# Second pair's slopes after the first pair's sine, its second chunk summed by a matrix of ones, and the copied product first

## The chip, the cores and the metric

The kernel runs on one core of one Trainium2 chip. The metric is the device time of one execution in microseconds; lower is better. The engines are named as the profile names them: PE is TensorE's matmul, PEld its weight load, DVE is VectorE, ACT is ScalarE, POOL is GpSimd, and SP issues the DMAs.

## The reference, cut to what matters

```python
# attention: a decayed linear recurrence per (batch, head), 768 steps, head size 48
mag = sqrt(a_re^2 + a_im^2);  scale = min(mag, 0.999) / (mag + 1e-6)
a = (a_re + i a_im) * scale
for t in range(768):
    S = a[t] * S + outer(k[t], v[t])        # S complex, the outer product real
    y[t] = q[t] @ real(S)
# first expert layer: 1536 tokens, 384 -> 2048 -> 384, softplus between
x = softplus(y_rows @ w_in) @ w_out
# second expert layer: 4 experts, 384 -> 1024 -> 384, relu between, weighted by p
out = sum_e p[:, e] * (relu(x @ w1[e]) @ w2[e])
```

The kernel does the recurrence in chunks of 128 steps: phases and log magnitudes are summed along time by a matmul with a triangular matrix, and a chunk is then scores, a mix with V, and a state for the next chunk.

## The kernel before

There are two batches of six chunks. A **pair** n is two chunks, c = 0 and 1, that share their activations: pairs 0 to 2 are batch 0, pairs 3 to 5 batch 1. One pair's front is: `squares` (L533: two squares on ScalarE, their sum on VectorE for pair 0, on GpSimd for the others), `ratio` (L539: Ln and Exp on ScalarE, then four VectorE operations that give a slope), `arctan` (L555), `logmag` (L548: Ln, Exp and two VectorE operations), `prefix` (L559: sums along time on TensorE), `wrap` and `level` (L587, L593: the results out of PSUM), `trig` (L623: Abs and two Sin). `decay` (L637) and `s3_units` (L645) then form the scaled queries and keys, transpose them on TensorE, and compute the chunk.

`prefix(n, c, what)` sums angles (what = 0) or log magnitudes (what = 1). For pair 0 the second chunk gets the first chunk's total from an additional matmul with a matrix of ones (L582). For all others `carry` (L603) fetches the last row of the chunk before with two small DMAs, and a GpSimd addition puts it into the first row of the next chunk (L564) before the triangular matmul. `s2_units` (L611) lists this chunk after chunk.

Ln and Exp lie in one table of ScalarE, Sin and Arctan in another. `excursion` (L717) loads the second table, runs what it is given, and loads the first one again. Before the change the first excursion holds the arctan of pairs 0 and 1 and the sine of pair 0 (`trigs0`, L777); the second one holds the sine of pair 1 and the arctan of pair 2.

What the program text says is put into each engine's own row by a scheduler at build time. An engine then works through its row in order: an instruction that waits holds up all behind it. Since the scheduler decides, some instructions stand elsewhere than the text has them.

From about 50 us on, the tokens go through the expert layers, in products of 128 x 384 on TensorE. Six of the twelve steps (`FAST`, second half of the run) use a form with eleven products in place of twelve (`part`, L407): four in q == 0 (px, two into pc, pv), three in q == 1, two in q == 2 and two in q == 3. In q == 0 ScalarE copies pc to `ha` (L437) and pv to `he` (L441), and VectorE adds px to `ha` (L438). The first product of q == 1 adds into pv, so it waits for the copy `he`; the third adds into px, so it waits for the addition to `ha`. A second-layer product (nine matmuls, L319) stands between two parts. Checks of the inputs (`look`, `look_w`, L887 and L901) run beside this: a DMA into a buffer of the ring `raw`, two ScalarE operations (L906, L907), one on VectorE. Weight loads use the same ring of four.

Of the kernel before, what the change touches and what calls it, by code (L numbers as in the profile page):

```python
# [15 lines left out]
ALU = mybir.AluOpType  # L16
# [59 lines left out]
def fast_path(ctx: ExitStack, tc, bad, wsc, qkv, a_re, a_im, w_in, w_out, probs, w1, w2, out):  # L76
    nc = tc.nc
# [327 lines left out]
    grp = {}  # L405

    def part(k, j, q):  # L407
        b = k // 6
        raws, sums = W[k, 2 * j]

        def prod(ps, w, x, start=False, stop=False):
            lt, li = (raws, w) if w < 5 else (sums, w - 5)
            for n, (p, r) in enumerate(((0, 0), (1, 0), (0, 1))):
                rhs = XC[b][:, r, x, :] if isinstance(x, int) else halves(b, *x, r)
                nc.tensor.matmul(ps, lt[:, p, li, :], rhs, start=(start and n == 0), stop=(stop and n == 2),  # L415
                                 skip_group_check=True)

        def keep(nm):
            return late["u"].tile([P, WM], F32, tag="h", name=f"{nm}{k}_{j}", bufs=3)

        def activate(f, blk, h):
            nm = f"{k}_{blk}_{f}"
            pool = tmp if blk == 0 else late["g"]
            g = pool.tile([P, 2, WM], F32R, tag="g", name="g" + nm, bufs=GB)
            nc.scalar.activation(g[:, 0, :], h, AF.Relu)
            nc.vector.scalar_tensor_tensor(g[:, 1, :], h, 0.0, g[:, 0, :].bitcast(F32), ALU.max, ALU.subtract)
            g_t[k, blk, f] = g

        if q == 0:
            x = grp["x"] = psum.tile([P, 512], F32, tag="h", name=f"px{k}_{j}", bufs=2)[:, :WM]  # L430
            c = psum.tile([P, 512], F32, tag="a", name=f"pc{k}_{j}", bufs=3)[:, :WM]
            v = grp["v"] = psum.tile([P, 512], F32, tag="a", name=f"pv{k}_{j}", bufs=3)[:, :WM]
            prod(x, 7, (1, 0), True, True)
            prod(c, 3, 0, True)
            prod(c, 4, (2, 0), False, True)
            h = keep("ha")
            nc.scalar.copy(h, c)  # L437
            nc.vector.tensor_tensor(h, x, h, ALU.add)  # L438
            prod(v, 9, (0, 1), True, True)
            e = grp["e"] = keep("he")  # L440
            nc.scalar.copy(e, v)  # L441
            activate(2 * j + 1, 0, h)
        elif q == 1:
            x, v = grp["x"], grp["v"]
            prod(v, 0, 3)
            prod(v, 2, (2, 0), False, True)
            h = keep("hb")
            nc.scalar.copy(h, v)
            prod(x, 8, 2, False, True)
            nc.vector.tensor_tensor(h, x, h, ALU.add)  # L450
            activate(2 * j, 0, h)
        elif q == 2:
            x, e = grp["x"], grp["e"]
            prod(x, 2, (2, 1))
            prod(x, 1, 4, False, True)
            nc.vector.tensor_tensor(e, x, e, ALU.add)
            activate(2 * j, 1, e)
        else:
            x = grp["x"]
            prod(x, 5, (2, 1))  # L460
            prod(x, 6, 1, False, True)
            activate(2 * j + 1, 1, x)
# [70 lines left out]
    def squares(n, sl):  # L533
        R, I, T1, T2 = (wide(t, sl) for t in st[n])
        nc.scalar.activation(T1, R, AF.Square)
        nc.scalar.activation(T2, I, AF.Square)
        (nc.vector if n == 0 else nc.gpsimd).tensor_tensor(T2, T1, T2, ALU.add)

    def ratio(n, sl):  # L539
        R, I, T1, T2 = (wide(t, sl) for t in st[n])  # L540
# [14 lines left out]
    def arctan(n):  # L555
        I = wide(st[n][1], slice(0, 2))
        act(I, I, AF.Arctan)

    def prefix(n, c, what):  # L559
        cc = (CH[n] + c) % CB  # L560
        src = st[n][1 if what == 0 else 3]
        if cc > 0 and n != 0:
            row = src[0:1, c, :]
            nc.gpsimd.tensor_tensor(row, rows[0][0:1, what, :], row, ALU.add)  # L564
        ps = psum.tile([P, 512], F32, tag="a", name=f"{'pf' if what == 0 else 'pl'}{n}_{c}", bufs=3)
# [11 lines left out]
            st[n, c, what] = ps  # L577
            return nc.tensor.matmul(ps[:, :HD], tri_r, lo, start=False, stop=True)
        t, lo = ((trik, onek), (tri, ones))[what]
        prev = range(c) if n == 0 else ()  # L580
        for i in prev:
            nc.tensor.matmul(ps[:, :HD], lo, src[:, i, :], start=(i == 0), stop=False)  # L582
        mm = nc.tensor.matmul(ps[:, :HD], t, src[:, c, :], start=(len(prev) == 0), stop=True)
# [25 lines left out]
        nc.sync.dma_start(rows[0][0:1, 1, :], dlam[127:128, :])  # L609

    def s2_units(n):  # L611
        units = []
        for c in range(2):
            units.append(lambda c=c: (prefix(n, c, 0), prefix(n, c, 1)))
            units.append(lambda c=c: (wrap(n, c), level(n, c)))
            if (CH[n] + c) % CB < CB - 1:
                units.append(lambda c=c: carry(n, c))
        return units
# [98 lines left out]
    def excursion(*parts):  # L717
        def run():
            use_table(TRIG)
            for f_ in parts:  # L720
                f_()
            use_table(LOGEXP)
        return run

    both = slice(0, 2)
# [43 lines left out]
        ratio(0, one[c])  # L769
    level(0, 0)  # L770
    decay(0, 0)
    squares(1, both)
    ratio(1, both)
    level(0, 1)
    decay(0, 1)

    def trigs0():  # L777
        arctan(0)
        for c in range(2):
            prefix(0, c, 0)  # L780
            if c == 0:
                arctan(1)
            wrap(0, c)
            if c == 1:
                carry(0, 1)
            trig(0, one[c])

    excursion(trigs0)()

    base = [0] + [24 + 16 * i for i in range(12)]  # L790
    ring = []
# [357 lines left out]
```

## Time and profile before

| | |
|---|---|
| median of 3 runs | 737.78 us (737.22 to 738.26) |
| the profiled execution | 738.36 us |
| its span, first to last instruction | 736.6 us |
| mean granted clock of TensorE | 0.988 of full |
| PE busy / PEld busy | 95% / 92% |
| DVE busy / ACT busy / POOL busy | 80% / 66% / 4% |

A page of the profile gives busy time by engine; the trace gives each instruction with its start, its duration, the idle time of its engine just before it, and what ended that. A busy share is an average over stages. This run has three: a start in which TensorE has little to do, a stretch in which attention and the first expert layer are mixed, and a long one of expert layers.

### The profile page before, as it was taken

To read this page: it belongs to the slowest core of one execution; us is meant where nothing else is said; L and a number is where in the kernel's file an instruction comes from. 1 tells how busy PE (TensorE), PEld (TensorE's weight loads), DVE (VectorE), ACT (ScalarE), POOL (GpSimd) and SP (SyncE) were. 2 spreads that over 40 slices of the span, in tenths; PEclk is the share of its full clock that TensorE was granted. 3 is DMA by queue.
4 is the path that set the end of the run, shared out by engine and by line. 5 is a ranking of instruction groups with operands and counts; after the bars stand their busy time and mean duration, and the time that the engine had idled before them with its cause. 6 is when DMAs were issued, how large, how long until landed. Compare 5 with 4: busy or idle time off the path is not lost.

```text
span 736.6 us, 13285 instructions
## 1 busy us (share of the span) xinstructions
PE 702.5 (95%) x5159; PEld 674.9 (92%) x5159; DVE 586.4 (80%) x1149; ACT 487.4 (66%) x898; POOL 32.3 (4%) x31
## 2 busy tenths in 40 slices
PE   2789999999999999999999999999999999999996
PEld 1468899999899999999999999999999999999996
DVE  6999999955875854548888779988778898998963
ACT  7887976888896856345686665555556567766640
POOL 1122010000111001000000000000000000000000
PEclk9699999999999999999999999999999999999998
DMA  7665666621211420121022120213445345455401
GB/s 268 195 191 179 201 203 192 224 77 44 86 45 59 122 80 2 59 86 44 23 86 65 43 87 21 87 44 109 119 157 155 127 151 172 150 172 152 162 31 69
DMA packets 36342, 83.56 MB, mean 113 GB/s; under 512 B 4528, under 2 KB 13232, under 8 KB 36272
## 3 DMA queue, kind: packets, MB, share of 16 engines
q1 hardware_dynamic: 36272, 82.64, 35.5%
q8 instruction: 42, 0.69, 0.4%
q14 instruction: 28, 0.23, 0.1%
HBM read 73.95 MB, written 8.65 MB: 112 GB/s over the span
## 4 chain that ended last, share of the span: by engine, by line


## 5 line engine op out<-in xcount | busy, mean ns | idle before, releaser
L232 PE MATMUL h<-X,A 128*128 128x384 f32 (+1 forms) x936 | 175.9, 329 | 2.3 <-ACT A L181 0.8
L232 PEld LDWEIGHTS h<-X,A 128*128 128x128 f32 x936 | 153.4, 188 | 5.6 <-issue 1.6
L319 PE MATMUL y<-B,g 128*128 128x384 f32 x744 | 150.2, 335 | 0.2 <-DVE acc L350 0.2
L319 PEld LDWEIGHTS y<-B,g 128*128 128x128 f32 x744 | 131.0, 188 | 0.7 <-issue 0.5
L319 PE MATMUL y<-g,B 128*128 128x384 f32 (+1 forms) x504 | 91.0, 315 | 0.3 <-ACT g L285 0.3
L319 PE MATMUL z<-B,g 128*128 128x384 f32 x372 | 84.7, 334 | 0.0
L319 PEld LDWEIGHTS y<-g,B 128*128 128x128 f32 x504 | 79.3, 189 | 2.0 <-ACT g L285 0.6
L319 PEld LDWEIGHTS z<-B,g 128*128 128x128 f32 x372 | 66.3, 188 | 0.0
L247 ACT ACTIVATE e<-h 128x384 f32<-128x384 f32 (+1 forms) x60 | 30.8, 512 | 37.1 <-PE h L232 36.0
L250 DVE SCALAR_TENSOR_TENSOR e<-h,e 128x384 f32<-128x384 f32 (+1 forms) x60 | 34.9, 581 | 20.6 <-ACT e L103 19.8
L255 DVE SCALAR_TENSOR_TENSOR g<-h,g 128x384 fp32r<-128x384 f32 x32 | 17.7, 555 | 28.1 <-ACT g L254 28.1
L103 ACT ACTIVATE e<-e,b_one 128x384 f32<-128x384 f32 (+1 forms) x60 | 38.2, 637 | 1.3
L103 ACT ACTIVATE e<-e 128x384 f32<-128x384 f32 (+1 forms) x60 | 32.8, 547 | 1.3
L415 PE MATMUL px<-X,sA 128*128 128x384 f32 x144 | 33.4, 340 | 0.0
L319 PE MATMUL z<-g,B 128*128 128x384 f32 x144 | 32.9, 335 | 0.0
L415 PE MATMUL px<-XC,sA 128*128 128x384 f32 x144 | 32.8, 336 | 0.0
L664 PE MATMUL tp<-ident,QK 128*96 128x128 f32 x192 | 27.2, 288 | 5.7 <-DVE QK L655 4.6
L664 PEld LDWEIGHTS tp<-ident,QK 128*96 128x96 f32 x192 | 22.2, 133 | 10.3 <-DVE QK L655 6.2
L254 ACT ACTIVATE g<-h 128x384 fp32r<-128x384 f32 x32 | 15.6, 488 | 21.3 <-PE h L232 21.1
L286 DVE TENSOR_TENSOR g<-e,g 128x384 fp32r<-128x384 f32 x48 | 26.6, 555 | 3.7 <-ACT g L285 2.9
L480 ACT CAST B<-rawB 128x768 fp32r<-128x768 f32 x24 | 20.0, 834 | 14.4 <-DMA rawB<-in_w_dram 7.3
L350 DVE SCALAR_TENSOR_TENSOR acc<-y,pr,acc 128x384 f32<-128x384 f32 x46 | 26.3, 612 | 1.7 <-PE y L319 1.7
(204 smaller groups left out, 1416.7 us busy)
## 6 DMA issues: line engine op xcount, KB each, us to landing
rawA<-in_w_dram SPq DMA_DIRECT2D x32, 384.0 KB, 3.0
rawB<-in_w_dram SPq DMA_DIRECT2D x32, 384.0 KB, 3.1
rawA<-in_w_in_dram SPq DMA_DIRECT2D x16, 384.0 KB, 3.5
rawB<-in_w_out_dram SPq DMA_DIRECT2D x16, 384.0 KB, 3.8
chkw<-in_w_in_dram SPq DMA_DIRECT2D x16, 384.0 KB, 3.2
chkw<-in_w_out_dram SPq DMA_DIRECT2D x16, 384.0 KB, 3.2
qk<-in_qkv_dram SPq DMA_DIRECT2D x12, 384.0 KB, 3.4
v<-in_qkv_dram SPq DMA_DIRECT2D x12, 256.0 KB, 2.9
```

Of the source, the lines that this page charges most:

```text
L103: i = nc.scalar.activation(out_, in_, fn, **kw)
L232: nc.tensor.matmul(ps, wt[:, p, kk, o:o + P], XB[b][:, q, kk, tok], start=(n == 0), stop=(n == 3 * KT - 1))
L247: nc.scalar.activation(t, h, AF.Abs)
L250: nc.vector.scalar_tensor_tensor(t, h, 0.0, t, ALU.max, ALU.add)
L254: nc.scalar.activation(g[:, 0, :], h, AF.Relu)
L255: nc.vector.scalar_tensor_tensor(g[:, 1, :], h, 0.0, g[:, 0, :].bitcast(F32), ALU.max, ALU.subtract)
L286: nc.vector.tensor_tensor(g[:, 1, :], t, g[:, 0, :].bitcast(F32), ALU.subtract)
L319: mm = nc.tensor.matmul(ys[j], l_, r_, start=(opens and n == 0 and not mate), stop=(closes and n == 2), skip_group_check=k == 0)
L350: nc.vector.scalar_tensor_tensor(dst, ys[j], pcol, dst, ALU.mult, ALU.add)
L415: nc.tensor.matmul(ps, lt[:, p, li, :], rhs, start=(start and n == 0), stop=(stop and n == 2), skip_group_check=True)
L480: nc.scalar.copy(hi, src)
L664: nc.tensor.transpose(tp[:96, hh, :], src[:, hf * 4 + hh, :], ident)
```

## The change

Three things change.

- `squares(1)` and `ratio(1)` move behind the first excursion, and `arctan(1)` gets an excursion of its own behind them: two more loads of ScalarE's tables. The sum of pair 1's squares moves from GpSimd to VectorE.
- Pair 1's second chunk gets the first chunk's total by a matmul with ones, as pair 0 does. Its two GpSimd row additions and the `carry` between its two chunks go. `s2_units(1)` now takes both chunks at a time: both angle sums, both wraps, both magnitude sums, both levels, one carry.
- In `part`, q == 0, the product pv and its copy `he` come ahead of px, pc and `ha`. This applies to the 24 groups of the six FAST steps.

```diff
 part, q == 0:
+            prod(v, 9, (0, 1), True, True)
+            e = grp["e"] = keep("he")
+            nc.scalar.copy(e, v)
             prod(x, 7, (1, 0), True, True)
             prod(c, 3, 0, True)
             prod(c, 4, (2, 0), False, True)
             h = keep("ha")
             nc.scalar.copy(h, c)
             nc.vector.tensor_tensor(h, x, h, ALU.add)
-            prod(v, 9, (0, 1), True, True)
-            e = grp["e"] = keep("he")
-            nc.scalar.copy(e, v)
             activate(2 * j + 1, 0, h)
 squares:
-        (nc.vector if n == 0 else nc.gpsimd).tensor_tensor(T2, T1, T2, ALU.add)
+        (nc.vector if n < 2 else nc.gpsimd).tensor_tensor(T2, T1, T2, ALU.add)
 prefix:
-        if cc > 0 and n != 0:
+        if cc > 0 and n != 0 and (n, c) != (1, 1):
-        prev = range(c) if n == 0 else ()
+        prev = range(c) if n < 2 else ()
 s2_units:
+        if n == 1:
+            return [lambda: (prefix(1, 0, 0), prefix(1, 1, 0)), lambda: (wrap(1, 0), wrap(1, 1)),
+                    lambda: (prefix(1, 0, 1), prefix(1, 1, 1)), lambda: (level(1, 0), level(1, 1)),
+                    lambda: carry(1, 1)]
 the start:
     decay(0, 0)
-    squares(1, both)
-    ratio(1, both)
     level(0, 1)
     decay(0, 1)
 trigs0:
             prefix(0, c, 0)
-            if c == 0:
-                arctan(1)
             wrap(0, c)
     excursion(trigs0)()
+    squares(1, both)
+    ratio(1, both)
+    excursion(lambda: arctan(1))()
```

Two places where the engines' rows change. The first is ScalarE's row between the last decays of pair 0 (`dec_1`) and the second pair's arctan. Names: `im_121` and `im_130` are the slopes of pairs 0 and 1, `t_131` and `t_132` pair 1's work tiles, `pf` an angle sum, `qT` and `kT` the transposed queries and keys, `t_485` (before: `t_488`) a work tile of pair 2. Before:

```order
L597 COPY zl_128<-pl_1_159 128x384
L103 ACTIVATE t_131<-t_131,b_tiny 128x768
L103 ACTIVATE t_131<-t_131 128x768
L103 ACTIVATE dec_1_189<-zl_128 128x384 x2
L97 ACT_TABLE_LOAD
L103 ACTIVATE im_121<-im_121 128x768
L181 CAST A_0_351<-fA_0_0_383 128x384
L590 ACTIVATE t_122<-pf_0_195,b_magic 128x384
L103 ACTIVATE im_130<-im_130 128x768
```

After, from the last Sin of pair 0 on:

```order
L97 ACT_TABLE_LOAD
L103 ACTIVATE t_131<-t_131,b_tiny 128x768
L669 COPY qT_0_0_230<-tp_0_0_231 96x512
L103 ACTIVATE t_131<-t_131 128x768
L97 ACT_TABLE_LOAD
L669 COPY kT_0_0_237<-tp_0_0_238 96x512
L669 COPY qT_0_1_244<-tp_0_1_245 96x512
L181 CAST B_0_470<-fB_0_1_488 128x384
L669 COPY kT_0_1_251<-tp_0_1_252 96x512
L536 ACTIVATE t_485<-im_483 128x768
L181 CAST A_1_498<-fA_1_0_503 128x384
L103 ACTIVATE im_130<-im_130 128x768
```

Pair 1's Ln, Exp and arctan have left the row ahead of pair 0's sines; they now stand among the copies of pair 0's transposes, with a load of the table on either side, and behind one square of pair 2.

The second place is TensorE's row from the transposes (`tp`) of pair 0 to its first scores (`sp`). Before:

```order
L664 MATMUL tp_0_0_236<-ident,QK_0_221 96x128 x4
L583 MATMUL pf_0_243<-im_130,trik 128x384
L664 MATMUL tp_0_1_249<-ident,QK_0_221 96x128 x4
L664 MATMUL tp_0_1_256<-ident,QK_0_221 96x128 x4
L664 MATMUL tp_1_0_338<-ident,QK_1_325 96x128 x4
L664 MATMUL tp_1_0_345<-ident,QK_1_325 96x128
L583 MATMUL pl_0_246<-t_132,tri 128x384
L673 MATMUL sp_0_0_263<-qT_0_0_228,kT_0_0_235 128x128 x4
```

After:

```order
L668 MATMUL tp_0_0_238<-ident,QK_0_223 96x128 x4
L668 MATMUL tp_0_1_245<-ident,QK_0_223 96x128 x4
L668 MATMUL tp_0_1_252<-ident,QK_0_223 96x128 x4
L668 MATMUL tp_1_0_342<-ident,QK_1_328 96x128 x4
L668 MATMUL tp_1_0_349<-ident,QK_1_328 96x128 x4
L583 MATMUL pf_0_259<-im_130,trik 128x384
L582 MATMUL pf_1_261<-im_130,onek 128x384
L583 MATMUL pf_1_261<-im_130,trik 128x384
L677 MATMUL sp_0_0_265<-qT_0_0_230,kT_0_0_237 128x128 x4
```

Pair 1's angle sums, now three matmuls in a row, stand right ahead of pair 0's first scores.

In the FAST steps one group shows the third change. This is ScalarE's row around the copies of a group whose copy `he` stood behind two operations of a check. Before:

```order
L480 CAST B_1_6464<-rawB_1_6462 128x768
L906 ACTIVATE chkv_6494<-chkw_6493 128x384
L437 COPY ha_3_6410<-pc_3_6399 128x384
L907 ACTIVATE chkv_6494<-chkv_6494,b_mid 128x384
L441 COPY he_3_6416<-pv_3_6400 128x384
L425 ACTIVATE g_0_7_6418<-ha_3_6410 128x384
L480 CAST A_2_6516<-rawA_2_6514 128x384
```

After:

```order
L480 CAST B_1_6461<-rawB_1_6459 128x768
L435 COPY he_3_6401<-pv_3_6397 128x384
L909 ACTIVATE chkv_6491<-chkw_6490 128x384
L910 ACTIVATE chkv_6491<-chkv_6491,b_mid 128x384
L440 COPY ha_3_6412<-pc_3_6396 128x384
L425 ACTIVATE g_0_7_6415<-ha_3_6412 128x384
L480 CAST A_2_6513<-rawA_2_6511 128x384
```

The copy `he` now stands ahead of the check; the copy `ha` stands behind it. The cast of the next weights follows in both.

## Rows read from the trace of the kernel before

**Rows 1.** The page, busy time of TensorE: us (share of span) xinstructions.
```profile
PE 702.5 (95%) x5159; PEld 674.9 (92%) x5159; DVE 586.4 (80%) x1149; ACT 487.4 (66%) x898; POOL 32.3 (4%) x31
```

**Rows 2.** Stages: us, busy of PE, PEld, DVE, ACT, POOL, PEclk, DMA share, GB/s.
```profile
50.00:115.00 65.00, 60.94 (x778) 54.89 (x779) 63.72 (x113) 50.78 (x92) 8.87 (x6) 1.00 0.62 194
430.00:730.00 300.00, 299.04 (x1705) 295.52 (x1703) 254.64 (x535) 173.10 (x341) 0.00 (x0) 1.00 0.37 116
```

**Rows 3.** Timeline at the start: start, us, engine, line, operation [idle before <- releaser].
```profile
11.86 2.10 POOL L537 TENSOR_TENSOR t<-t,t 128x768 f32<-128x768 f32 x1 [10.13 <-ACT t L536]
12.33 2.04 DVE L545 TENSOR_TENSOR im<-im,re 128x384 f32<-128x384 f32 x1
12.83 0.48 ACT L597 COPY zl<-pl 128x384 f32<-128x384 f32 x1 [0.22 <-PE pl L583]
...
13.99 0.94 ACT L103 ACTIVATE t<-t,b_tiny 128x768 f32<-128x768 f32 x1 [0.69 <-POOL t L537]
...
14.96 0.84 ACT L103 ACTIVATE t<-t 128x768 f32<-128x768 f32 x1
...
16.77 1.28 ACT L97 ACT_TABLE_LOAD   x1
...
18.06 0.84 ACT L103 ACTIVATE im<-im 128x768 f32<-128x768 f32 x1
...
18.96 1.65 PE L583 MATMUL pf<-im,trik 128*128 128x384 f32 x2 [6.17 <-ACT im L103]
...
26.41 1.94 PE L664 MATMUL tp<-ident,QK 128*96 128x128 f32 x8 [3.42 <-DVE QK L655]
```

**Rows 4.** ScalarE alone, from arctan to decays: us, busy, PEclk, DMA share, GB/s.
```profile
18.06:51.00 32.94, 28.76 (x46) 0.83 0.60 184
```

**Rows 5.** Timeline around the first scores of the first pair.
```profile
27.88 1.19 POOL L564 TENSOR_TENSOR im<-rows,im 1x384 f32<-1x384 f32 x1 [13.93 <-DMA rows<-tail]
...
33.82 0.91 PE L583 MATMUL pl<-t,tri 128*128 128x384 f32 x2
...
34.57 1.95 PE L673 MATMUL sp<-qT,kT 96*128 96x128 f32 x16
...
36.07 1.82 POOL L537 TENSOR_TENSOR t<-t,t 128x768 f32<-128x768 f32 x1 [2.30 <-ACT t L536]
```

**Rows 6.** The granted clock there, microsecond by microsecond; columns as in rows 2.
```profile
32.00:33.00 1.00, 1.00 (x7) 0.96 (x6) 0.94 (x2) 0.96 (x3) 0.22 (x1) 0.53 0.88 267
33.00:34.00 1.00, 0.82 (x5) 0.38 (x4) 0.53 (x2) 0.97 (x3) 0.77 (x1) 1.00 0.87 237
```

**Rows 7.** Timeline at the first expert matmuls and second pair's decays.
```profile
49.00 0.74 PE L232 MATMUL h<-X,A 128*128 128x256 f32 x4 [0.72 <-ACT X L711]
...
49.71 1.28 ACT L97 ACT_TABLE_LOAD   x1
...
51.00 0.94 ACT L103 ACTIVATE dec<-t 128x384 f32<-128x384 f32 x2
...
55.31 1.96 PE L664 MATMUL tp<-ident,QK 128*96 128x128 f32 x16 [1.23 <-DVE QK L655]
```

**Rows 8.** Timeline, VectorE's waits after that and TensorE's last long one.
```profile
73.26 1.03 DVE L182 TENSOR_TENSOR B<-fB,B 128x384 fp32r<-128x384 f32 x2 [0.51 <-ACT B L181]
86.83 0.56 DVE L182 TENSOR_TENSOR B<-fB,B 128x384 fp32r<-128x384 f32 x1 [0.37 <-ACT B L181]
114.07 0.59 PEld L689 LDWEIGHTS yps<-A,v 128*32 128x32 f32 x24 [1.33 <-DVE A L674]
```

**Rows 9.** Waits of PEld, 430 to 600 us (total, times, longest); then the timeline.
```profile
PEld pv L415 <- ACT he L441: 1.8, 4, 0.7
...
566.55 0.55 ACT L906 ACTIVATE chkv<-chkw 128x384 f32<-128x384 int32 x1 [1.36 <-DMA chkw<-in_w_in_dram]
570.25 0.51 ACT L480 CAST A<-rawA 128x384 fp32r<-128x384 f32 x1 [1.48 <-DMA rawA<-in_w_dram]
571.88 0.48 PEld L415 LDWEIGHTS px<-X,A 128*128 128x128 f32 x3 [0.39 <-DVE hb L450]
```

## The prediction, made before the changed kernel ran

> **What bounds the kernel now.** I read the page first, for the engine with most busy time: TensorE, 95% [rows 1]. That is an average, so next come the stages. From 115 us on TensorE hardly waits; in the FAST steps it is busy 299.04 of 300 us [rows 2]. There, time can be gained only where it still waits. From 50 to 115 us VectorE is busy 63.72 of 65 us and TensorE 60.94 [rows 2]: VectorE is the tighter one, and the last long wait of TensorE, 1.33 us before 114.07, is for VectorE's mask of the scores [rows 8]. What is early or late there reaches the end in full, since nothing behind it has slack. Before 50 us TensorE waits for ScalarE and VectorE: 6.17 us for the arctan, 3.42 us for the scaled queries [rows 3]. So I ask when VectorE and TensorE come into the full stretch, that is, when the second pair's decays run (51.00) and when the first expert matmul does (49.00) [rows 7], and then what FAST gives.
>
> All sums are made against the profiled execution, 738.36 us, of which 736.6 are its span. It lies 0.58 above the median of the runs, 737.78; I carry the difference over to the median.
>
> **What is taken out before the first sine.** After the copy at 12.83 and the first pair's decays, ScalarE runs Ln (0.94) and Exp (0.84) of the second pair, the Ln after a wait of 0.69 for GpSimd's sum of squares, then the load of the table [rows 3]. Now the decays are followed by the load. The copy ends at 13.3; two decays take 0.94 [rows 7], the load 1.28: the first arctan starts at 15.5 and not at 18.06, 2.5 us earlier. VectorE has its input by then: the instruction at 12.33 took 2.04 us because GpSimd's sum ran until 13.96, and ended 0.41 after it [rows 3]; in its place stands the sum itself on VectorE, an operation with 768 columns that I estimate at 1 us from the 0.94 of such an activation [rows 3]. The 2.5 us go on through the angle sums, sines and products: the first transposes, at 26.41 before [rows 3], come at about 23.9.
>
> **What comes back behind it.** The moved work stands among the copies of those transposes. ScalarE from the first arctan to the second pair's decays was busy 28.76 us of 32.94 [rows 4], so it waited 4.2. The new row adds Ln and Exp (1.78) and two loads (2.56), and loses the copy for the removed carry (short, 0.48 like the copy at 12.83 [rows 3]): 28.76 + 3.86 = 32.6. Without waits the decays would run at 15.5 + 32.6 = 48.1, 2.9 us earlier than now. All turns on the waits.
>
> On the loads a row and a rule differ. The row: after the load at 49.71 the next activation starts at 51.00 [rows 7], and after that at 16.77 at 18.06 [rows 3], 1.29 us each time. The Trainium skill, page "ScalarE: Activation LUTs", section "What ACT_TABLE_LOAD costs", has 1283 ns for the load and some 1380 ns more for a drain, 2.66 us for each switch, and its rules ask to group activations by table, which this change does not. By the row the two loads cost 2.6 us, by the page 5.3; I take the row.
>
> The waits. Until the first wrap of an angle sum two casts of weights now stand ahead of it, and they wait for VectorE's chain of conversions, which takes as long as before: I estimate 2.5 us of waits in all up to the second arctan. That arctan ends at 34.3 by the same account: 15.5, twenty-two operations, two loads, and these waits. Its result isn't at TensorE then. GpSimd has first to add the carried row to the first chunk (1.19 [rows 5]), and ahead of it in GpSimd's row stands the sum of the third pair's squares (1.82 and 2.10 [rows 3, 5]), which waits for a square that ScalarE ends only at about 33.1, just ahead of the cast and the arctan. So GpSimd is done at 33.1 + 1.9 + 1.2 = 36.2. Then TensorE runs three matmuls of the angle sums in a row, of which the one with ones is new, and behind them the first pair's scores. At the lower level of the clock (1.2 GHz) three such passes took from 18.96 to 22.99, 4.0 us (the end by the idle 3.42 ahead of the transposes at 26.41) [rows 3]; at the upper (2.4 GHz) one took 0.91 [rows 5], three some 2.1 since they overlap. Scores begin at 40.2 or at 38.3; before, they began at 34.57 [rows 5]. Which level? Before, TensorE restarted at 26.41 and was granted half until the last part of 32 to 33 and the full clock after [rows 6]. Now it has before 36.2 only pieces of transposes, with waits for copies between them, and 2.5 us of nothing just ahead. I take the lower level.
>
> ScalarE meanwhile: after the arctan the load and a Ln, to 36.5. It waits for the first angle sum until 36.2 + 1.65 = 37.85 (1.3 us), runs a wrap and an Exp, and waits for the second until 40.2 (1.0). With 2.5 from above these are 4.8 us of waits: 48.1 + 4.8 = 52.9 for the second pair's decays against 51.00, **1.9 us late**. At the upper clock the two waits for angle sums are 0.5 and not 2.3: 51.1, no change. The lead is given back either way.
>
> From there VectorE has full rows again. It can catch up only where it waited before: 0.51 at 73.26 and 0.37 at 86.83 [rows 8], 0.9 in all. So at 114.07 it is 1.0 us late, and TensorE with it: **+1.0**. Bounds: the 2.9 early, of which TensorE's waits after 50 us take some 2 (the 1.33, and part of the rest of 65 - 60.94): -2.0. On the other side, the first expert matmul, whose input is cast by ScalarE behind the last load, would start at 53.0 and not at 49.00; if all but the 1.23 us wait at 55.31 [rows 7] stays, +2.8.
>
> **Ones in place of a carry.** Two matmuls more (one for angles, in the sum above; one for magnitudes, which runs while ScalarE loads a table: 0). Gone are two additions of one row on GpSimd (about 1.2 each [rows 5]), during which VectorE's operations stall as at 12.33 [rows 3], a tail copy (counted) and two small DMAs. What VectorE saves lies in the stretch in which it now waits for ScalarE anyway: 0. If it were the bound there, -2, which is the lower bound above. SP's row has two entries less ahead of weight loads; those land long before their use: 0.
>
> **The product pv first.** In FAST TensorE's weight loads waited 1.8 us, four times, for the copy `he` [rows 9]. Now the copy is ready three matmuls earlier, and in all four places it stands ahead of the cast or check operation which waited for a DMA. Those waits go. But ScalarE still waits in its row for the same DMAs, and what it copies after them is next: at 570.25 the cast of weights waits 1.48 us for its load, the copy `hb` follows, and TensorE waits 0.39 for it at 571.88 [rows 9]. If TensorE is 0.7 us earlier there it waits 0.7 longer. Gain 0 to 1.8, I take **-0.5**, a little over a quarter: one of the four has no such gate close behind. The copy `ha` is now later by three matmuls, 0.53 us at 1705 in 300 us [rows 2], and px must wait for the addition to it; at worst +0.5.
>
> **Sum.** +1.0 - 0.5 = +0.5 us: 738.9 for an execution like the profiled one, **738.3** for the median. From the bounds: 737.8 - 2.0 - 1.8 = 734.0 to 737.8 + 2.8 + 0.5 = 741.1.
>
> **The rivals.**
> *Faster: the lead is kept and the waits for `he` go in full.* The place is the angle sum at 36.2: if it comes earlier, since GpSimd is free earlier or the clock is up, ScalarE's waits shrink by 2 us and VectorE keeps what it no longer loses to GpSimd. For it: VectorE's saving is real, and 1.33 us at 114.07 wait for it. Against: GpSimd's order. Price -1.0 at the start and -1.5 in FAST: 735.3.
> *Slower: TensorE takes VectorE's place as the bound between 50 and 115 us.* The first expert matmul starts 4 us late, and TensorE has 60.94 us of work in those 65. It decides if that matmul starts after about 52, since then the waits that lateness could fill are used up. For it: those waits stand before copies and casts which are late, too. Against: eight matmuls of that first product now stand behind the transposes at 55.31, so these don't wait for them. +2.8 - 0.5: 740.1.
> *The loads cost twice what they take.* If behind each added load ScalarE stood still as long again, 1.28 us, the decays would be 2.6 us later: 740.9. The two loads with an activation right behind them [rows 3, 7] speak against it. The page cited above would have it so.
>
> **How the numbers follow.** A measurement of this kernel tells about 0.2%, 1.5 us, from no change. The forecast, within that of 737.8, gets 0.43; its own range is 736.3 to 739.3. The faster rival gets 0.29, the slower one 0.27, the loads 0.01. So faster 0.29, same 0.43, slower 0.28. The range leaves a tenth at each end: into the faster case down to 735.0, into the slower up to 740.7.
>
> **What would show each step.** First arctan at 15.5, first transposes at 24, with the Ln and Exp after the load. The first pair's scores at about 40, behind three angle matmuls, at half clock, and GpSimd's row addition ending at 36. The second pair's decays at 51 to 53. TensorE's wait at about 114 moved by about 1 us. In FAST no wait of pv for `he`, and longer ones of px for `hb` where the DMA comes late. I am wrong if the scores come before 38, if the decays come before 50, or if what is late at 53 has vanished by 114; and in FAST if the waits for `hb` do not grow.

## The result, and the profile after

| | before | changed |
|---|---|---|
| median, run side by side | 737.63 us (737.22 to 738.26) | 743.67 us (743.30 to 744.32) |
| a second set (e14) | 738.98 us (737.33 to 741.12) | 745.91 us (743.55 to 747.72) |
| the profiled execution, and its span | 738.36, 736.6 us | 743.30, 741.6 us |

The ratio is 1.0078 (95% interval 1.0057 to 1.0098); in the second set 1.0087 (1.0066 to 1.0108). The change makes the kernel **about 6 us slower**. The forecast was 738.3 with a range up to 740.7: wrong. Differences below are the ratio times the median of before of the same set.

The page of the changed kernel, and the stages of [rows 2] with the first 50 us ahead of them:

```profile
PE 702.2 (95%) x5163; PEld 676.8 (91%) x5163; DVE 584.6 (79%) x1150; ACT 489.4 (66%) x899; POOL 32.4 (4%) x28
```
```profile
0.00:50.00 50.00, 24.67 (x153) 15.90 (x154) 38.62 (x79) 38.22 (x62) 5.31 (x11) 0.76 0.68 221
50.00:115.00 65.00, 59.93 (x816) 54.35 (x816) 62.09 (x111) 53.84 (x96) 13.27 (x6) 1.00 0.56 178
430.00:730.00 300.00, 299.60 (x1716) 297.65 (x1715) 258.93 (x548) 179.91 (x352) 0.00 (x0) 1.00 0.37 117
```

The work is the same as in [rows 1], to half a microsecond on TensorE. What changed is when it is done: from 50 to 115 us TensorE has 59.93 us of work (60.94 in [rows 2]), VectorE 62.09 (63.72). In the FAST steps TensorE is busy 0.56 us longer in the same 300 us.

The start, to set beside [rows 3] (start, us, engine, line, operation, idle before and what ended it):

```profile
15.57 0.94 ACT L103 ACTIVATE dec<-zl 128x384 f32<-128x384 f32 x2 [1.59 <-DVE qk L647]
16.52 1.28 ACT L97 ACT_TABLE_LOAD   x1
17.82 0.84 ACT L103 ACTIVATE im<-im 128x768 f32<-128x768 f32 x1
...
26.10 1.63 PE L668 MATMUL tp<-ident,QK 128*96 128x128 f32 x8 [3.18 <-DVE QK L659]
```

The first arctan starts at 17.82, not at 15.5. The second pair of decays of the first pair waits 1.59 us, because `dec` has one buffer and VectorE frees it with the product at L647. One of the first loads landed later in this profile than in that of before, and the first magnitude sum starts at 9.79 in place of 8.82 (in all other profiles here at 9.30 to 10.05). From that sum to the arctan it takes 8.03 us, and 9.24 before: 1.2 us of lead where 2.5 were forecast.

The stretch that [rows 5] show of before:

```profile
31.03 1.28 ACT L97 ACT_TABLE_LOAD   x1
32.33 0.58 ACT L669 COPY kT<-tp 96x512 f32<-96x512 f32 x1
...
35.72 0.84 ACT L103 ACTIVATE im<-im 128x768 f32<-128x768 f32 x1
36.58 1.28 ACT L97 ACT_TABLE_LOAD   x1
...
41.80 0.58 ACT L590 ACTIVATE im<-pf,b_magic 128x384 f32<-128x384 f32 x1 [3.00 <-PE pf L582]
```
```profile
32.96 2.85 PE L668 MATMUL tp<-ident,QK 128*96 128x128 f32 x12 [1.55 <-ACT kT L669]
38.78 1.65 PE L583 MATMUL pf<-im,trik 128*128 128x384 f32 x2 [2.96 <-POOL im L564]
40.22 1.49 PE L582 MATMUL pf<-im,onek 128*128 128x384 f32 x2
41.50 1.49 PE L583 MATMUL pf<-im,trik 128*128 128x384 f32 x2
42.78 2.31 PE L677 MATMUL sp<-qT,kT 96*128 96x128 f32 x16
```
```profile
35.50 1.96 POOL L537 TENSOR_TENSOR t<-t,t 128x768 f32<-128x768 f32 x1 [33.77 <-ACT t L536]
37.42 1.31 POOL L564 TENSOR_TENSOR im<-rows,im 1x384 f32<-1x384 f32 x1
```

The scheme of the forecast is there: two table loads among the transposes' copies, the row addition of GpSimd behind the third pair's sum, three angle passes at half the clock, the scores behind them. But the scores start at 42.78, not at 40.2 (before 34.57). The first wrap (41.80) waits 3.00 us, for the second of the three passes and not for the first: it writes over the first chunk's angles (`wrap` puts its result where they lie), and the matmul with ones still reads them. The clock, to set beside [rows 6], and ScalarE alone from arctan to decays, beside [rows 4]:

```profile
40.00:41.00 1.00, 1.00 (x3) 0.48 (x2) 0.56 (x2) 0.00 (x0) 0.00 (x0) 0.50 1.15 254
...
43.00:44.00 1.00, 1.00 (x8) 1.00 (x8) 0.56 (x1) 0.60 (x2) 0.00 (x0) 0.73 0.81 243
```
```profile
17.82:56.17 38.35, 32.10 (x49) 0.71 0.56 179
```

TensorE was granted half (1.2 GHz) all through the angle passes, and more only from 43 us on; before, from 33. The stretch of [rows 7]:

```profile
54.51 1.28 ACT L97 ACT_TABLE_LOAD   x1
...
56.17 0.94 ACT L103 ACTIVATE dec<-t 128x384 f32<-128x384 f32 x2
```
```profile
56.33 3.84 PE L232 MATMUL h<-X,A 128*128 128x256 f32 x29 [0.76 <-ACT X L715]
...
95.65 0.98 PE L232 MATMUL h<-X,A 128*128 128x256 f32 x6 [2.07 <-DVE e L250]
...
132.44 0.39 PE L260 MATMUL gs<-g,one_r 128*128 128x256 f32 x1 [1.20 <-ACT g L275]
```

Decays and first expert matmul are 5.2 and 7.3 us later than before (4.2 and 6.4 counted from the first magnitude sum). Hardly anything of it is made good. Counted from the first magnitude sum, TensorE is 6.36 us late at the first expert matmul, 4.64 at the one matmul at L260 that lies in the first block, and 6.25 at the first FAST product: what it catches up by 70 us goes in new waits, 1.22 us for GpSimd at 79.36 and those at 95.65 and 132.44. Ahead of the last one VectorE waits, for the DMA that stores converted weights and frees one of the two buffers `f`; before, it has no such wait there:

```profile
128.98 0.36 DVE L70 TENSOR_SCALAR fB<-rawB 128x384 int32<-128x384 int32 x1 [2.21 <-DMA moe_weights<-fA]
```

In FAST, the waits of the weight loads, 430 to 740 us (total, times, longest), to set beside the first line of [rows 9]:

```profile
PEld y L319 <- DVE acc L350: 0.7, 1, 0.7
PEld px L415 <- DVE hb L450: 0.3, 1, 0.3
PEld px L415 <- DVE ha L441: 0.3, 1, 0.3
```

The four waits of pv for `he` are gone, one of px for `ha` has come.

### The profile page after: what moved, and what is told of

Read it like the earlier page. It is cut to its first block, busy times and chain, and to the rows that moved or that the text cites. A ratio compares the mean times of both kernels' runs of the same rounds, so it can differ in the third digit from the quotient of the medians.

```text
span 741.6 us, 13293 instructions
## 1 busy us (share of the span) xinstructions
PE 702.2 (95%) x5163; PEld 676.8 (91%) x5163; DVE 584.6 (79%) x1150; ACT 489.4 (66%) x899; POOL 32.4 (4%) x28
## 4 chain that ended last, share of the span: by engine, by line
## 5 line engine op out<-in xcount | busy, mean ns | idle before, releaser
L250 DVE SCALAR_TENSOR_TENSOR e<-h,e 128x384 f32<-128x384 f32 (+1 forms) x60 | 34.8, 580 | 21.1 <-ACT e L103 20.1
```

What stands on the lines that cost most here:

```text
L250: nc.vector.scalar_tensor_tensor(t, h, 0.0, t, ALU.max, ALU.add)
```

## The experiments

Four sets of four and one of two, each beside the kernel before. The last column counts from the first magnitude sum, less the same in the profile of before; FAST is the first of its products. That column comes from one execution each: e1 has the rows of before up to FAST and is at -1.03 there, so about 1 us of it is spread.

| kernel | against before, us (95%) | late at first scores / first expert matmul / FAST |
|---|---|---|
| changed | +5.8 (4.2 to 7.2), +6.4 (4.9 to 8.0) | 7.24 / 6.36 / 6.25, again 7.05 / 5.92 / 7.72 |
| e1 FAST order alone | -1.0 (-1.9 to 0.0) | -0.02 / -0.03 / -1.03 |
| e2 moved slopes alone | +8.5 (6.9 to 10.1) | 11.08 / 11.76 / 8.70 |
| e3 ones alone | +6.1 (4.3 to 7.8) | 0.05 / 2.73 / 5.43 |
| e4 sum on VectorE alone | 0.0 (-1.1 to 1.0) | -0.61 / -0.61 / -1.14 |
| e5 scores first | +3.3 (1.8 to 4.7) | -1.53 / 1.68 / 4.61 |
| e7 third sum on VectorE | +5.1 (3.5 to 6.8) | 5.32 / 4.94 / 6.75 |
| e9 VectorE's work twice | +3.4 (2.1 to 4.7) | 0.77 / 0.58 / 4.64 |
| e10 ScalarE's work twice | +4.2 (3.1 to 5.3) | 2.73 / 2.20 / 2.03 |
| e11 four passes more | +7.1 (5.5 to 8.6) | 1.49 / 5.25 / 5.31 |
| e12 scores first, later list | +5.9 (4.8 to 7.1) | -1.33 / 3.05 / 6.95 |
| e13 changed, one addition first | +5.2 (4.0 to 6.5) | 7.55 / 6.30 / 6.57 |
| e15 ones' list, no passes | -2.1 (-3.0 to -1.3) | -1.03 / -0.33 / -1.26 |
| e16 ones, one addition first | +3.8 (2.5 to 5.2) | -0.48 / 2.22 / 4.11 |
| e17 changed, no passes | +2.7 (1.7 to 3.7) | 6.32 / 5.37 / 4.99 |
| e18 ones, table load late | -0.1 (-1.3 to 1.0) | -0.94 / -1.06 / 0.13 |

### Each part alone

e1: in `part`, q == 0, only.

```diff
+            prod(v, 9, (0, 1), True, True)
+            e = grp["e"] = keep("he")
+            nc.scalar.copy(e, v)
             prod(x, 7, (1, 0), True, True)
```

> The kernel before with only the copied product pv and its copy first in the eleven-product groups. The changed kernel was 6.0 us slower, and its lateness against before shrank from 7.7 us at the first px of the FAST steps to 5.4 us at the last. Theory 'FAST gives 2': the reorder alone is 1.8 to 2.3 us faster than before, and no weight load of pv waits for he. Theory of the prediction, with waits for hb in their place: 0.5 us faster, waits for hb longer by 1 us or more. Rival 'the 2.3 us are only slack that soaked up a late start': no change, within 0.4 us.

737.75 us: 1.0 faster, between the prediction's 0.5 and the 2 that I read from the trace of the changed kernel. Its waits for `he` are gone; `ha` costs 0.7 and `hb` 0.9 us (before 0.6):

```profile
PEld px L415 <- DVE hb L450: 0.9, 3, 0.4
PEld px L415 <- DVE ha L441: 0.7, 2, 0.4
```

It is the version to keep: some 7 us faster than the changed kernel, and 0 to 1.9 faster than before, an interval that touches no change.

e2: the slopes moved, nothing else.

```diff
-    squares(1, both)
-    ratio(1, both)
...
-            if c == 0:
-                arctan(1)
...
     excursion(trigs0)()
+    squares(1, both)
+    ratio(1, both)
+    excursion(lambda: arctan(1))()
```

> The kernel before with only the second pair's squares, slopes and arctan behind the first sine, in an excursion of their own; the sum on GpSimd, the row additions and the carry chunk by chunk stay. Theory M, the moved slopes and their two table loads among the transposes' copies cost all of the 7.4 us at the start: 5.5 to 9 us slower, first scores later than 40 us, first expert matmul at 54 to 58. Rival O, the cost comes from summing both chunks at a time ahead of the scores: not over 3 us slower, scores before 38.

746.92 us: 8.5 slower, theory M by its numbers. Listed chunk by chunk, the magnitude sum stands ahead of the scores too, and waits for GpSimd's second row addition, which waits for VectorE's `t` behind the Ln and Exp after the added loads:

```profile
39.34 1.65 PE L583 MATMUL pf<-im,trik 128*128 128x384 f32 x2 [2.97 <-POOL im L564]
45.04 1.65 PE L583 MATMUL pl<-t,tri 128*128 128x384 f32 x2 [4.05 <-POOL t L564]
46.48 3.62 PE L673 MATMUL sp<-qT,kT 96*128 96x128 f32 x16
```

e3: the matmul with ones and the list for both chunks, nothing else.

```diff
-        prev = range(c) if n == 0 else ()
+        prev = range(c) if n < 2 else ()
...
+        if n == 1:
+            return [lambda: (prefix(1, 0, 0), prefix(1, 1, 0)), lambda: (wrap(1, 0), wrap(1, 1)),
+                    lambda: (prefix(1, 0, 1), prefix(1, 1, 1)), lambda: (level(1, 0), level(1, 1)),
+                    lambda: carry(1, 1)]
```

> The kernel before with only the matmul with ones for the second pair's second chunk and its list of units for both chunks at a time; the slopes stay ahead of the first sine, the sum of squares on GpSimd. Theory M: within 1 us of before, first scores within 1 us of 34.57 plus one pass of an angle sum (0.9 to 1.3 us). Rival O: 4 to 8 us slower, with scores behind two more angle matmuls and the first expert matmul at 52 or later.

744.31 us: 6.1 slower, by the time rival O; but not for its reason, since the scores are 0.05 us late. So M, which put the whole cost on the move, falls too: each half costs about as much as both together. The time is lost at the second chunk's transposes (below, e18), and at 90 us.

e4: `n < 2` for `n == 0` in `squares`.

> The kernel before with only the sum of the second pair's squares on VectorE instead of GpSimd. Theory: the instruction of VectorE at 12.33, which took 2.04 us beside GpSimd's sum, falls to about 0.55, the sum itself takes 0.95 as in the changed kernel; the Ln that waited 0.69 us for GpSimd waits less; the first arctan starts 0 to 0.7 us earlier and the whole is 0 to 0.7 us faster. Rival 'the sum stands ahead of the first pair's product with the decays and holds the decay buffer': the second decays wait 1 us or more for VectorE, first arctan later than 18.06, whole 0.3 to 1.5 us slower.

738.31 us: no difference, the lower end of the theory. The instruction that took 2.04 us takes 0.56, the sum 0.96, and the first angle sum comes 0.92 us earlier; so the lead of the changed kernel comes mostly from this part (e2, without it, has none: 0.07 later).

### Does the order of TensorE's row make it late?

e5 and e12 are the changed kernel with two or one empty entries in the list, which puts the second pair's angle sums behind the first pair's scores.

```diff
-    put([lambda: logmag(1, both)] + s2_units(1) + ...
+    put([lambda: logmag(1, both)] + [lambda: None] * 2 + s2_units(1) + ...
```

> The changed kernel with two empty entries put behind the second pair's magnitudes in the list that sets the order, so that TensorE's row has the first pair's scores, mix and state ahead of the second pair's angle sums. Theory 'the scores stand behind angle sums that aren't ready': scores start at 36 to 37 instead of 42.78, the first expert matmul at 49 to 52 instead of 56.33, and the whole is 3 to 6 us faster than the changed kernel (before plus 0 to 3). Rival 'ScalarE's row with two more table loads sets the pace whatever TensorE does first': less than 2 us faster than the changed kernel, that is 4 us or more slower than before.

742.95 us, 2.5 to 3 less than the changed kernel. It can't be taken at its word: with two entries the second pair's products with the queries come ahead of its sine, so they don't wait for it and take its argument in its place. e12 has one entry and keeps the order.

> The changed kernel with one empty entry behind the second pair's magnitudes in the list that sets the order: in TensorE's row the first pair's scores and the second chunk's first transposes come ahead of the second pair's angle sums. Theory V: the scores come at 34 to 36 instead of 42.78, but VectorE's waits from 18 to 134 stay between 6 and 10 us (10.01 in the changed kernel), and the whole is 0.5 to 3 us faster than the changed kernel, still 3 us or more slower than before. Rival, the scores behind angle sums are the whole cost: within 1 us of before or faster.

744.49 us, as slow as the changed kernel, though the scores come 8.6 us and the first expert matmul 3.3 us earlier. The rival falls. The wait goes elsewhere, to VectorE for the Exp of the third pair, and to TensorE for the product of VectorE behind it:

```profile
47.98 0.96 DVE L543 TENSOR_TENSOR re<-re,t 128x768 f32<-128x768 f32 x1 [3.10 <-ACT t L103]
60.81 3.24 PE L668 MATMUL tp<-ident,QK 128*96 128x128 f32 x16 [2.80 <-DVE QK L659]
```

e7: `n < 3` in `squares` of the changed kernel.

> The changed kernel with the sum of the third pair's squares on VectorE too, so that GpSimd has nothing ahead of the row addition for which the angle sums wait. Theory: that addition starts when the arctan ends, at about 36.6 instead of 37.42, the angle sum starts at 37.8 instead of 38.78, and the whole is 0.5 to 1.5 us faster than the changed kernel. Rival 'VectorE loses as much by the sum': within 0.4 us of the changed kernel.

744.82 us, +5.1: the angle sum starts at 37.86 as expected, the first matmul 1.0 to 1.4 us earlier, and at FAST it is as late as the changed kernel (6.75; 6.25 and 7.72). The theory's local times held; whether 0.7 us of the end is gained, the intervals don't tell.

e6 and e8 list the chunks one by one but keep the matmul with ones.

> The kernel before with only the matmul with ones for the second pair's second chunk, and its units listed chunk by chunk as before (without the carry between them). The same with both chunks at a time cost 6 us. Theory 'the list for both chunks at a time costs, since three angle sums and three magnitude sums come ahead of the second chunk's transposes': within 1 us of before, first expert matmul 30 to 31 us after the first angle sum, as before. Rival 'the two more matmuls, some 2 us of TensorE at half clock, cost': 2 to 6 us slower.

> The changed kernel with the second pair's units listed chunk by chunk (matmul with ones kept). The first magnitude sum, which waits for GpSimd's second row addition behind the Ln and Exp after a table load, then stands ahead of the scores, where it waited 4.05 us in the kernel with the moved slopes alone. Theory M2: scores at 45 or later, 1 to 3 us slower than the changed kernel. Rival 'chunk by chunk is the better order here too': faster than the changed kernel by 2 us or more, as in the kernel with early slopes.

8645 and 8656 us; they answer nothing. `wrap` and `level` write their results over what was summed, and in this list that comes before the matmul with ones reads it. With such sums the kernel's guard on its own values takes its slow, general path. What follows is that the list for both chunks isn't a choice: the matmul needs it, unless the result gets a tile of its own.

### What does a microsecond of each engine cost there?

Three probes on the kernel before: repeated work whose result isn't needed early.

```diff
+            for _ in range(2 if k == 0 and n < 3 else 1):
+                nc.vector.tensor_tensor(lo, src, hi.bitcast(F32), ALU.subtract)
...
+            for _ in range(2 if k == 0 and n < 3 else 1):
+                nc.scalar.copy(hi, src)
...
+        if n == 1:
+            nc.tensor.matmul(ps[:, :HD], lo, src[:, c, :], start=True, stop=True)
```

The first is e9, the second e10, the third e11.

> The kernel before with six subtractions of the first weights (128x384, 0.55 us each as one, about 0.48 in a row) done twice on VectorE, between 20 and 50 us: 2.8 to 3.3 us of work on nobody's way, whose result isn't needed before 49. Theory V, VectorE is the bound from the first sine to 130 us (it waits 3.44 us from 18 to 134 before, 10.01 in the changed kernel): 2.0 to 3.3 us slower. Rival, TensorE's or ScalarE's row is the bound in the start: within 1 us of before.

741.83 us, +3.4: as theory V had it by its number. The first expert matmul is only 0.6 us late; the wait comes behind it:

```profile
59.15 3.62 PE L665 MATMUL tp<-ident,QK 128*96 128x128 f32 x16 [3.83 <-DVE QK L656]
```

> The kernel before with the six casts of the same weights done twice on ScalarE: 6 x 0.52 = 2.5 to 3.1 us more of ScalarE between 20 and 50 us, about as much as two table loads (2.56). Theory V: ScalarE has waits to spare (1.47 for the third pair's sum, 0.55, 0.20 and what lies ahead of the first matmul), so 0 to 1.5 us slower. Rival A, ScalarE's row with the added table loads is what makes the changed kernel late: 2.5 us slower or more.

742.82 us, +4.2: rival A, not V. ScalarE's waits were not to spare.

> The kernel before with one matmul pass more ahead of each of the second pair's four angle and magnitude sums (overwritten by the sum): four passes of 0.65 us at the full clock or 1.28 at half, 2.6 to 5.1 us more of TensorE between 28 and 45 us. The changed kernel has two such passes more. Theory V: the scores come 1 to 3 us later, VectorE has other rows meanwhile, 0 to 1.5 us slower. Rival P, TensorE's passes ahead of the scores cost in full: 2.6 us slower or more.

745.84 us, +7.1: rival P, not V. So none of the three theories holds as "the engine that bounds the start". About 3 us on any one of the three costs 3.4 us or more. Work passes from one to the next and each has the other's result behind its own row. But these are not prices of the work alone. In all three the scheduler built other rows: in e9 and e10 up to some 53 us (the load of the sines' table, ahead of one copy of the second chunk's transposes in before, stands ahead of three in e9 and behind all four in e10), in e11 beyond 100 us too, where TensorE waits 2.06 us for the addition at L250, as below.

And in e9 TensorE lost its clock. It was granted half from 57.5 to 64.3 us, from within its wait of 3.83 us on, and before has the full clock there. Four microseconds of it in e9, then in before:

```profile
60.00:64.00 4.00, 4.00 (x20) 3.88 (x19) 2.15 (x4) 2.94 (x6) 1.23 (x1) 0.50 0.35 98
```
```profile
60.00:64.00 4.00, 4.00 (x99) 2.92 (x88) 4.00 (x10) 3.82 (x7) 0.62 (x1) 1.00 0.56 163
```

The sixteen transposes at 59.15 take 3.62 us in place of 1.96 in [rows 7]. TensorE is busy for the last 5.1 us of that stretch, so by estimate up to 2.6 of the 3.4 us are the clock's.

### The passes, or the order that comes with them?

In every late kernel with the ones, and in e11, TensorE waits 1.5 to 2.1 us at 93 to 96 us for VectorE's addition at L250, and none in before, e1, e4, e9 or e10. (e2, without the ones, waits 1.30 us at 97.80.) VectorE's row there has three conversions and a product with decays ahead of it, which stood behind it before. e13 and e16 tie these behind the addition.

```diff
+            if (k, n, h) == (1, 0, 0):
+                behind(i, emitted[0, 0, 7])
```

> The changed kernel with VectorE's row altered from 91 us on alone: the addition of the first layer's last features of the first block (at L250 before) stands right behind the cast of the weights ahead of it, as in the kernel before, and not behind three conversions and a product with the decays. Theory 'the 2.07 us wait of TensorE before 95.65 is a loss of its own': that wait is gone, the lateness at the end of the attention falls from 7.5 to 5.4, 1.2 to 2.2 us faster than the changed kernel in e14. Rival 'VectorE is the bound there, and what it puts off it owes': the wait reappears by 135 us, within 0.6 us of e14.

> The changed kernel again, beside the others of this set: 5 to 7 us slower than before.

> The kernel with the ones alone (e3, 6 us slower), with the same addition put first in VectorE's row at 90 us. Theory 'a loss of its own': 1.2 to 2.2 us faster than e3, 4 to 5 slower than before. Rival: within 0.6 us of e3.

744.42 against 745.91 us (1.2 less by the ratios), and 743.91 for e16 (2.2 less than e3, in another set). All intervals overlap, so a gain of 1 to 2 us is likely and not shown. The wait itself did not go as expected. The addition now waits for ScalarE's Ln instead (but VectorE's wait for the DMA, 2.2 to 2.4 us in the changed kernel, its repetition and e3, is absent in both):

```profile
94.31 0.69 DVE L255 SCALAR_TENSOR_TENSOR e<-h,e 128x512 f32<-128x512 f32 x1 [1.83 <-ACT e L104]
95.05 1.34 PE L235 MATMUL h<-X,A 128*128 128x256 f32 x9 [1.66 <-DVE e L255]
```

e15 and e17 take the two passes out of e3 and of the changed kernel.

```diff
-        prev = range(c) if n < 2 else ()
+        prev = range(c) if n == 0 else ()
```

> The kernel with the ones alone (e3, 6 us slower than before), its list for both chunks at a time kept, but without the two matmuls with ones: the second chunk of the second pair leaves out the first chunk's totals, so the output isn't the reference's. Theory P, the two passes of TensorE (1.28 us at half clock and 0.65 at full) ahead of the scores and the second chunk's transposes cost: 2 to 4 us faster than e3, that is 2 to 4 slower than before. Rival L, the list for both chunks costs by itself: within 1 us of e3, that is 5 us or more slower than before.

> The changed kernel without the two matmuls with ones (the second pair's second chunk leaves out the first chunk's totals, so the output isn't the reference's). Theory 'the passes cost 6 to 8 us here too': before minus 2 to plus 1. Theory 'the moved slopes with two table loads cost by themselves, and the passes lie in waits': within 2.5 us of the changed kernel, that is 3.5 us or more slower than before.

e15: 736.87 us, 2.1 faster than before and 8.2 faster than e3. Theory P's sign was right and its size far too small: what takes 2 us of TensorE costs 8. (Without the passes the wraps don't wait for them either.) The list itself, with fewer additions on GpSimd and one carry less, is a gain. e17: 742.20 us, +2.7, between its two theories. In the changed kernel the passes cost 3.1 to 3.7 us. Less e1's gain, if the parts add up, the move with the list costs 3.7.

e18 is e3, with the load of the sines' table tied behind the four copies of the second chunk's transposes.

```diff
+                if (n, c) == (0, 1):
+                    copies.append(i)
...
+        + [lambda: tabs["since"].extend(copies), excursion(lambda: trig(1), lambda: arctan(2))], -8, 0)
```

> The kernel with the ones alone (e3, 6 us slower than before), in which the load of the table of sines comes behind the four copies of the second chunk's transposes, where it stands in the list without the passes. The wait of 2.16 us of TensorE for the copy goes. Theory 'the order cost most of it': 3 us or more faster than e3, within 3 us of before. Rival 'the passes cost by their time on TensorE': within 2 us of e3, 4 us or more slower than before.

739.09 us: no slower than before. **The order cost 6.2 of the 8.2 us**, the passes' own time about 2.0 (e15 at -2.1, e18 at -0.1). ScalarE in e3, then in e18:

```profile
42.83 1.28 ACT L97 ACT_TABLE_LOAD   x1
44.12 0.58 ACT L669 COPY qT<-tp 96x512 f32<-96x512 f32 x1
```
```profile
41.52 0.59 ACT L671 COPY qT<-tp 96x512 f32<-96x512 f32 x1
...
44.35 1.28 ACT L97 ACT_TABLE_LOAD   x1
```

and TensorE in both:

```profile
40.48 0.81 PE L582 MATMUL pl<-t,ones 128*128 128x384 f32 x2
...
44.75 0.64 PE L668 MATMUL tp<-ident,QK 128*96 128x128 f32 x4 [2.17 <-ACT qT L669]
```
```profile
39.47 0.81 PE L582 MATMUL pl<-t,ones 128*128 128x384 f32 x2
...
42.16 0.64 PE L670 MATMUL tp<-ident,QK 128*96 128x128 f32 x4 [0.59 <-ACT qT L671]
```

With the passes the transposes come later; presumably the copy isn't ready when the scheduler reaches it, and it takes the table load first. On the chip TensorE then waits 2.17 us for the copy in place of 0.59. That doesn't make 6. The tie also changed rows ahead of it (the second chunk's angle sum stands ahead of a group of transposes, and the first scores come 1.0 us earlier) and behind it: the wait before L250 at 93 us is absent in e18. So 6.2 us is the price of that load's place with all that the scheduler builds around it, not of the one wait.

The clock is in it, too. In e3 TensorE was granted half from 45.6 to 49.0 us, behind its wait of 2.17 us, and again from 93.4 to 96.7, behind that of 2.06; e18 has the full clock in both stretches. Three microseconds in e3, then in e18 (TensorE's matmuls in parentheses):

```profile
46.00:49.00 3.00, 3.00 (x20) 2.38 (x18) 2.60 (x5) 2.63 (x6) 0.00 (x0) 0.50 0.54 159
```
```profile
46.00:49.00 3.00, 2.83 (x101) 2.19 (x92) 2.93 (x7) 2.74 (x5) 0.49 (x1) 1.00 0.10 36
```

TensorE is busy all through both stretches in e3, so each costs it up to 1.7 us of work by estimate, half of 3.4: together up to 3.4 of the 6.2. The repetition of the changed kernel has such a stretch from 96.9 to 100.3, the first execution has none, and they come to FAST 7.72 and 6.25 us late.

## Why the prediction was wrong, step by step

**The lead of 2.5 us.** It came as 1.2. "VectorE has its input by then" followed the arctan's input alone; ScalarE has first to run the second decays, and their buffer is freed by a VectorE product at 15.5. The removed Ln and Exp filled a wait.

**What comes back behind it.** The work was right: 32.10 us of ScalarE from arctan to decays (forecast 32.6), and each load 1.28 with 0.01 or 0.02 behind it, as in [rows 3, 7]. The Trainium skill, page "ScalarE: Activation LUTs", section "What ACT_TABLE_LOAD costs", has some 1380 ns more for a drain: neither load above shows it. The waits were 6.25 us in place of 4.8, the start 2.3 later: decays at 56.17 in place of 52.9. From the first arctan to the second it took 17.9 us, as forecast (15.5 to 33.5; measured 17.82 to 35.72), so up to there all the lateness is that of the start. What the sum lacked lies behind: 3.00 us for the first wrap, which I had wait for one pass (2.3 for both sums), and 0.63 for the first copy behind the scores. GpSimd's order, the clock at half and the three passes were as told: 42.78 - 38.78 = 4.0.

**The step that failed most: "it can catch up", and the bound of +2.8.** The decays were 5.2 us late (4.2 from the first magnitude sum) in place of 1.9, and the FAST steps began 6.25 us late in place of 1.0. I took VectorE as the bound from 50 us on and summed what it could save in its waits. But what comes later is also built in another order, and there the waits are new: at 95.65 and 132.44, and that of VectorE for a DMA at 128.98. The slower rival had the mechanism, a first expert matmul too late to be absorbed, with "decides if it starts after about 52": it started at 56.33. Its price of 2.8 was less than half.

**"Ones in place of a carry: 0".** This is the term of the sum that was mis-sized by most: 3.1 to 3.7 us in the changed kernel, 8.2 with early slopes. I counted each pass beside the engine that waits at that moment. e9 to e11 show that some 3 us on none of the engines came free before 60 us, with the rows built anew. And the built order, which e18 shows to weigh three times as much as the passes in e3, I took only as a list of what lies ahead of what, with no price for a row that now stands badly, nor for the clock that falls behind the wait which it causes. How much of the 3.1 to 3.7 is order was not tried in the changed kernel, where the load of the sines' table stands ahead of two of the copies (47.84; copies at 50.76 and 51.23). That the removed additions and carry might be worth 2 us, which I left as a bound, is what e15 with the list alone gives (2.1).

**FAST: -0.5.** Right in kind, and inside its bounds: -1.0 (-1.9 to 0.0). pv's waits for `he` went, waits for `ha` and `hb` came. I had `he` ready three matmuls earlier; it is three products, nine matmuls. The trace of the changed kernel alone would have given 1.85, its repetition 0.17.

**The sum on VectorE, 1 us for 2.04 of a stalled instruction.** Right in the trace, worth nothing at the end.

What stays open: how the 3.7 us of the move divide between its work on ScalarE (32.10 in place of 28.76 us from arctan to decays; in e10 about 3 us more cost 4.2, rows built anew included), the order built with it, and the clock (half until 43 us, before until 33). No kernel here moves the slopes and keeps all other rows.

## What to carry to other kernels

Where three engines hand work to each other with short rows, don't price work on any of them at nothing because that engine has waits: three probes of some 3 us cost 3.4 to 7.1. Where a scheduler writes the rows, compare the rows at each wait of the bounding engine, above all where a table load or a row of conversions now stands ahead of a copy that another engine waits for: one tie that puts the copy first was worth three times the added work. And read the granted clock behind each new wait of TensorE before you put the whole loss on the wait.

## What the runs showed of the hardware

- Behind a wait of TensorE the granted clock can be half for a while, with TensorE busy all that time: in e9 in and behind 3.83 us, in e3 behind 2.17 and behind 2.06. It isn't so behind each: the changed kernel waits 2.07 us before 95.65 and keeps the full clock, and its repetition, after 2.06 us, does not.
- The clock that a profile lists for the start can't be taken at its word. In e11 two passes stand 1.28 us apart (21.40 and 22.68), which is the distance at half clock, where the list has 1.00. So a mean granted clock of 0.997 in place of 0.988 does not say that an execution's start ran faster:

```profile
21.40 1.49 PE L584 MATMUL pf<-im,onek 128*128 128x384 f32 x2
22.68 1.49 PE L585 MATMUL pf<-im,trik 128*128 128x384 f32 x2
```
```profile
21.00:24.00 3.00, 3.00 (x5) 1.11 (x4) 3.00 (x8) 2.20 (x5) 0.00 (x0) 1.00 0.62 197
```

- A float32 pass of 128x384 takes 0.65 us at full and 1.28 at half clock (the distance of starts above, 40.48 to 41.12 in e3 and 40.22 to 41.50 in the changed kernel).
- One execution's trace can mislead by more than what is sought: the changed kernel's FAST steps lasted 1.85 us less than before in one profile and 0.17 less in another, and 0.58 less in that of e18, which has the FAST steps of before.
